# First chunk of an attention and MLP kernel: two loads, masks ahead of the transposes, copies by tile, a third PSUM pair, and unread matmuls in every early gap

## The chip, the cores and the metric

The kernel runs on one core of a Trainium2 chip. Its engines are TensorE (PE, with its weight loads shown apart as PEld), VectorE (DVE), ScalarE (ACT), GpSimd (POOL) and SyncE (SP), and 16 DMA engines move data between HBM and the core's SBUF. Matmuls write to PSUM, which has eight banks of 512 fp32 columns by 128 partitions. The metric is the device time of one execution in microseconds, compared by the median of several runs.

## The reference

Four sequences (B = 4) of 768 positions with 8 heads of 64 go through attention with a window of 128 and 4 sink positions, and then through an MLP over rows of 512:

```python
scores = scale * np.matmul(q, k.transpose(0, 1, 3, 2))
keep = is_sink | in_window                 # first 4 positions, or 0 <= rel < 128
scores = np.where(keep, scores, -1000000000.0)
a = softmax(scores); attn = np.matmul(a, v)
x = attn as [B, S, 512]
xn = (x - mean) / sqrt(var + 1e-6) * g_ln
out = x + np.maximum(xn @ w_ch1, 0.0) @ w_ch2     # w_ch1 512x2048, w_ch2 2048x512
```

Inputs and output are fp32; inside, nearly everything is bf16 with fp32 accumulation.

## The kernel before, in words

**Tiles and chunks.** A tile is 128 query positions of one sequence, a chunk is two tiles (256 positions); there are 12 chunks, three to a sequence. A tile attends to its own 128 keys, to the 128 before them, and, from the third tile on, to the 4 sinks apart. A chunk goes through these stages: loads of k, q and v (POOL issues them, with a cast to bf16), transposes of k and q so that head channels lie on partitions (`kq`), scores, `exp` on ACT, a mask, value matmuls, normalisation and the LayerNorm statistics on DVE, the transpose of the centred rows (`xc` to `xnt`), and two MLP matmuls with a ReLU between them. The MLP weights (`w1`, `w2`, four blocks each) are loaded once, behind the loads of the first chunks.

**The start.** The first four chunks are transposed by PE (`by_dma=4`), later ones by the DMA. For those, `n4` holds k on 64 partitions and q on the other 64, and `tr` (L588 to L593) transposes four heads at a time into one PSUM bank (`pt`, ring `one`), which `evict` (L557) copies to `kq` in one operation of 1024 columns, on ACT or DVE. Chunk 0's loads are cut in half by heads, so that the four loads are k and q of heads 0 to 3, then of heads 4 to 7. Chunks 0 and 1 go through `attend_tile` (L618) tile by tile; from chunk 2 on, `attend` (L670) takes both tiles at once. For tiles 0 and 1 the mask is added in PSUM ahead of the scores: `mk` (L632) multiplies an identity with `neg`, which holds a large negative number where a position is not to be seen, and the scores accumulate on it. `neg` is made on DVE (L490 to L492) from `upper`, which POOL makes with an `affine_select` (L461) behind the first loads. From tile 2 on, the probabilities are multiplied with a 0/1 mask on DVE (L654). `sk` and `sx` (L657 to L663) are the scores of the sinks and their exp, one of each per tile for tiles 2 and 3.

**PSUM.** Two pairs of banks (`pair`) take scores and value sums, four single banks (`one`) the rest.

**What sets the order.** Every operation is recorded in `Plan` with the engines it may run on, a duration that the author gives it, a priority and its buffers. `Plan.run` (L113) lays all of them out in time by these durations: for each engine it picks, among operations that could start within `WINDOW` of the earliest, the one of lowest priority number. It also chooses ACT or DVE where both are possible, and the buffers from the rings. Each engine's instructions are then written in the order of these planned times, and the engine executes them in that order, waiting on semaphores. So a changed duration, priority or ring moves operations on every engine.

**Unread matmuls.** Ahead of 24 us of planned time, gaps of over 0.6 us in PE's plan are filled with matmuls of `junk` into a bank that is free then, whose result nobody reads (L974 to L996); they are 512 columns wide.

Of the kernel before, what the change touches and what calls it, by code (L numbers as in the profile page):

```python
# [7 lines left out]
FP32 = mybir.dt.float32  # L8
BF16 = mybir.dt.bfloat16
# [55 lines left out]
class Plan:  # L65
# [45 lines left out]
    WINDOW = {"PE": 0.4, "ACT": 0.25, "DVE": 0.25, "POOL": 0.25, "SP": 0.0}  # L111

    def run(self):  # L113
        free = {"PE": 0.9, "ACT": 0.75, "DVE": 0.9, "POOL": 1.05, "SP": 0.75}
# [103 lines left out]
SW_4 = (1.4, 0.7, 0.9)  # L218
SW_H = (0.7, 0.8, 0.9)
# [142 lines left out]
def kernel(  # L362
# [38 lines left out]
    pairs = [psum.tile([128, 2, 512], FP32, name=f"pair{i}") for i in range(2)]  # L401
    ones = [psum.tile([128, 512], FP32, name=f"one{i}") for i in range(4)]
    P.ring("pair", [Slot(pairs[i], f"pair{i}", banks[2 * i:2 * i + 2]) for i in range(2)])
    P.ring("one", [Slot(ones[i], f"one{i}", [banks[4 + i]]) for i in range(4)])
# [89 lines left out]
    constant("masks0", "DVE", 0.9, 6.1, masks0, ["upper"], writes=[Bc["mask0"]], nb=20.0)  # L494
# [49 lines left out]
    roots = {}  # L544
# [17 lines left out]
    def load4(c, nm, hs, prio, dma, writes):  # L562
        b, R = c // RC, c % RC
        p0 = 64 * "kq".index(nm)
        ap = (k if nm == "k" else q)[b, hs, 256 * R:256 * R + 256, :].rearrange("h (p i) d -> p h (i d)", i=4)
        P.op(f"{nm}ld{c}{hs.start}", {"POOL": (0.85, 0.9)}, prio, lambda e: G.dma_start(  # L566
            n4_b[c].t[p0:p0 + 64, hs].rearrange("p h i d -> p h (i d)"), ap), writes=writes + [n4_b[c]], dma=dma)

    def chunk(c):
# [5 lines left out]
        if c < PAR["by_dma"]:  # L575
            halves = [[Buf(f"l{c}{hh}{i}") for i in range(2)] for hh in range(2)]
            if c == 0:
                for hh in range(2):
                    for i in range(2):
                        load4(c, "kq"[i], slice(4 * hh, 4 * hh + 4), -110 + hh + 0.1 * i, SW_H, [halves[hh][i]])  # L580
            else:
                for i in range(2):
                    load4(c, "kq"[i], slice(0, H), (PAR["ld1"] if c == 1 else ld) + 0.01 * i, SW_4, [halves[0][i], halves[1][i]])
            for hh in range(2):
                pt, done = Buf(f"pt{c}{hh}", "one"), Buf(f"T{c}{hh}")
                tile_of[c, hh] = done

                def tr(e, pt=pt, hh=hh):  # L588
                    pb = pt.t.bitcast(BF16).rearrange("p (h k i g) -> p h i k g", h=2, k=2, i=4)
                    for h in range(2):  # L590
                        for i in range(4):
                            for h2 in range(2):
                                nc.tensor.transpose(pb[64 * h2:64 * h2 + 64, h, i], n4_b[c].t[:, 4 * hh + 2 * h + h2, i, :], ident)  # L593
                trs[c, hh] = P.op(f"tr{c}{hh}", pe(0.448 if c else 0.9), d + 0.02 + 0.1 * hh, tr, reads=halves[hh] + [Bc["ident"]],
                                  hold=[n4_b[c], T], writes=[pt], mode="c")
                evict(f"ev{c}{hh}", d + 0.05 + 0.1 * hh, 1024,
                      lambda pt=pt: pt.t.bitcast(BF16).rearrange("p (m i g) -> p m g i", m=4, i=4),
                      lambda hh=hh: T.t[:, 2 * hh:2 * hh + 2].rearrange("p h k (g i) -> p (h k) g i", i=4), [pt], [T, done], fp=True)
        else:
            for x, (nm, src) in enumerate((("k", k), ("q", q))):  # L600
                for i in range(2):
                    nat = Buf(f"{nm}n{c}{i}", "nat")
                    ap = src[b, :, 256 * R + 128 * i:256 * R + 128 * (i + 1), :].rearrange("h p d -> p h d")
                    P.op(f"{nm}ld{c}{i}", {"POOL": (0.87, 0.9)}, ld + 0.01 * i + 0.1 * x,
                         lambda e, nat=nat, ap=ap: G.dma_start(nat.t, ap), writes=[nat], dma=SW, after=behind(c))  # L605
                    P.op(f"tr{nm}{c}{i}", {"SP": (1.2, 1.2)}, d + 0.01 * i, lambda e, nat=nat, i=i, x=x: dma_t(
                        T.t[:, :, x, 128 * i:128 * i + 128], nat.t.rearrange("p h d -> p (h d)")),
                        reads=[nat], writes=[T], dma=HW_X, after=[scores[c - 1]])
        if R == 0:
# [4 lines left out]
                for h2 in range(2)], reads=[T], writes=[kts], after=kts_zero)  # L614
# [3 lines left out]
    def attend_tile(t):  # L618
# [4 lines left out]
        need = [[tile_of[cc, hh] for hh in ((j,) if t else (0, 1)) for cc in {c, (t - 1) // 2 if t else 0}]  # L623
                for j in range(2 if t else 1)]
        ps, pp_s = (Buf(f"ps{t}", "ps"), Buf(f"pss{t}", "one")) if c else (None, None)
        pes = []
        for j in range(2 if t else 1):
            pp, pb = Buf(f"s{t}{j}", "pair"), Buf(f"p{t}{j}", "pe")
# [8 lines left out]
            if t < PAR["pm"]:  # L637
                P.op(f"pm{t}{j}", pe(0.44), d + 0.06 + 0.1 * j, mk, reads=[Bc["neg"], Bc["ident"]], writes=[pp],
                     after=[trs[c, 0], trs[c, 1]])

            def sc(e, pp=pp, j=j):
                for hp in (range(2 * j, 2 * j + 2) if t else range(HP)):
# [6 lines left out]
            P.op(f"sc{t}_{j}", pe(0.25), d + 0.1 + 0.1 * j, sc, reads=need[j], **{"rw" if t < PAR["pm"] else "writes": [pp]},  # L649
                 hold=[kq, kprev, pb], mode="r")  # L650
# [5 lines left out]
        if c:  # L656
            def sk(e):  # L657
                for hp in range(HP):
                    nc.tensor.matmul(pp_s.t[32 * hp:32 * hp + 32, 0:128], lhsT=kts_b[0].t[:, hp, :],
                                     rhs=kq.t[:, hp, 1, own], start=True, stop=True, skip_group_check=True)  # L660
            P.op(f"sk{t}", pe(0.21), d + 0.15, sk, reads=[kq, kts_b[0]], writes=[pp_s], hold=[ps], mode="c")
            P.op(f"sx{t}", {"ACT": act(128)}, d + 0.16, lambda e: nc.scalar.activation(
                ps.t[:, own], pp_s.t[:, 0:128], AF.Exp, scale=scale), reads=[pp_s], writes=[ps])  # L663
# [58 lines left out]
    def value(c, i, pes, ps, d, part, srcs):  # L722
        b, R, t = c // RC, c % RC, 2 * c + i
        po = Buf(f"po{t}", "pair")
# [250 lines left out]
    t = 1.2  # L975
    for o in order:
        if o.eng != "PE":
            continue
        if o.start > 24.0:
            break  # L980
        n = int((o.start - t - 0.45) / (0.43 if t < 8 else 0.25))
        if n > 0 and o.start - t > 0.6:
            free = [(max([e_ for b_, e_ in banks[i].lives if b_ < t], default=0.0), i) for i in range(8)
                    if all(e_ < t or b_ > o.start + 0.3 for b_, e_ in banks[i].lives)]
            if free:
                i = min(free)[1]
                items.append((t + 0.001, -n, pairs[i // 2][:, i % 2, :] if i < 4 else ones[i - 4]))
        t = o.start + o.engs["PE"][0]
    items.sort(key=lambda z: (z[0], z[1]))
    with tc.manual_schedule():  # L990
        for _, s, o in items:
            if s < 0:
                for _ in range(-s):
                    nc.tensor.matmul(o, lhsT=junk[:, 0:128], rhs=junk, start=True, stop=True)
# [43 lines left out]
```

## Time and profile before

| what | value |
|---|---|
| median of three runs | 219.2 us (218.75 to 219.54) |
| the profiled execution | 218.84 us |
| its span, first to last instruction | 217.3 us |
| busy in the span: PE, DVE, ACT, POOL | 205.6, 157.1, 118.6, 84.8 us |
| landings of chunk 0's four loads | 5.26, 6.20, 7.13, 8.54 us |
| landings of chunk 1's k and q | 11.25, 13.00 us |
| landings of w1's four blocks | 16.07, 21.20, 23.74, 26.69 us |
| landings of w2's four blocks | 33.52, 35.74, 38.28, 41.01 us |
| first exp starts, first reciprocal starts | 12.13, 13.83 us |

A landing is the moment when a transfer's semaphore tells that all of its bytes are there; the trace gives it as the time from issue to landing. In a timeline row the columns are start and duration in us, engine, line of the code, operation, tiles written and read, shape, count, and in brackets the engine's idle time ahead of it with what ended it. In a row of busy time by stretch they are the stretch and its length, then for PE, PEld, DVE, ACT and POOL the busy us and the number of instructions, then the granted clock of PE, the busy share of the DMA engines and the GB/s that they moved. A chain row gives start, duration and who held the chain. Line numbers are those of the kernel before.

### The profile page before, as it was taken

The numbers are of one execution on the slowest core, as the hardware profiler recorded it, in microseconds if no ns is written. First come the engines' busy times: TensorE is split into PE (matmuls) and PEld (weight loads), VectorE is DVE, ScalarE is ACT, GpSimd is POOL, SyncE is SP. The second block draws the span as 40 slices with busy tenths as digits, with TensorE's granted clock in tenths as the row PEclk, the third lists the DMA queues.
The fourth block names the chain that finished last, engine by engine and source line by source line (L and its number), as shares of the span: only waits on it lengthen the run. The fifth ranks groups of instructions, "written<-read, shape, count | busy, mean of one in ns | idle before, by whom it ended". The sixth has DMA issues, their size and how long they took to land.

```text
span 217.3 us, 5914 instructions
## 1 busy us (share of the span) xinstructions
PE 205.6 (95%) x2378; PEld 167.8 (77%) x2383; DVE 157.1 (72%) x398; ACT 118.6 (55%) x180; POOL 84.8 (39%) x128
## 2 busy tenths in 40 slices
PE   6689999999999799999999999999999999999990
PEld 1447995684697698898897987987988988988880
DVE  3349953499899688689688697787786786794460
ACT  2379577258599756544565555555456456442600
POOL 7968473477039029039057066066110110110000
PEclk9999999999999999999999999999999999999997
DMA  5999999999949949989989939949943520222003
GB/s 48 143 182 202 201 192 207 187 194 147 203 79 108 174 101 90 135 175 99 158 134 130 170 93 140 216 35 141 165 113 48 148 48 0 100 48 94 7 3 109
DMA packets 98098, 26.97 MB, mean 124 GB/s; under 512 B 86800, under 2 KB 94992, under 8 KB 98064
## 3 DMA queue, kind: packets, MB, share of 16 engines
q0 software_dynamic: 66720, 13.64, 78.7%
q1 hardware_dynamic: 31344, 12.89, 31.3%
q8 instruction: 20, 0.33, 0.6%
q14 instruction: 14, 0.11, 0.2%
HBM read 27.30 MB, written 6.29 MB: 155 GB/s over the span
## 4 chain that ended last, share of the span: by engine, by line
PE 85%; DVE 4%; ACT 4%; DMA 2%; issue 1%; POOL 1%; DVEq 0%; ACTq 0%; POOLq 0%
PE one L806 32%; PE one L886 28%; PE one L837 5%; PE one L799 5%; PE pair L734 4%; PE pair L692 4%; DMA n<-in_q_dram 2%; PE pair L729 2%; ACT pe L651 1%; PE one L593 1%; ACT w L948 1%; DVE st L753 1%; POOL n L566 1%; ACT pe L706 1%; PE pair L634 1%
## 5 line engine op out<-in xcount | busy, mean ns | idle before, releaser
L816 ACT ACTIVATE hq<-one 128x512 bf16<-128x512 f32 x93 | 55.4, 598 | 56.1 <-PE one L806 44.9
L806 PE MATMUL one<-xnt,w 128*128 128x256 bf16 x640 | 74.5, 273 | 0.0
L806 PEld LDWEIGHTS <-w 128*128 128x128 bf16 x640 | 61.4, 98 | 7.1
L706 ACT ACTIVATE pe<-pair 128x1024 bf16<-128x1024 f32 (+1 forms) x40 | 36.4, 958 | 22.2 <-PE pair L692 22.2
L761 POOL TENSOR_SCALAR st<-st 128x1 f32<-128x1 f32 x24 | 6.2, 259 | 89.9 <-DVE rec L747 76.7
L886 PEld LDWEIGHTS <-hs 128*128 128x128 bf16 x320 | 30.0, 98 | 5.6 <-issue 1.3
L886 PE MATMUL one<-n,hs 128*128 128x256 bf16 x240 | 29.6, 273 | 0.0
L710 DVE TENSOR_TENSOR pe<-pe,mask 128x1024 bf16<-128x1024 bf16 (+1 forms) x40 | 24.9, 643 | 5.0 <-ACT pe L706 5.0
L900 DVE TENSOR_TENSOR tm<-one,x 128x256 f32<-128x256 f32 x40 | 16.8, 421 | 12.3 <-PE one L886 12.3
L886 PEld LDWEIGHTS <-hq 128*128 128x128 bf16 x240 | 23.3, 98 | 3.0 <-ACT hq L816 0.3
L553 POOL DMA_DIRECT2D vn<-in_v_dram x24 | 21.4, 906 | 4.5 <-DVE xc L764 1.9
L869 DVE TENSOR_TENSOR hs<-hq 128x512 bf16<-128x512 bf16 x40 | 15.4, 413 | 5.4 <-ACT hq L816 5.4
L886 PE MATMUL one<-w,hq 128*128 128x256 bf16 x160 | 19.3, 273 | 0.0
L907 DVE TENSOR_TENSOR ot<-one,tm 128x256 f32<-128x256 f32 x40 | 16.7, 417 | 1.3 <-PE one L886 1.1
L749 DVE TENSOR_TENSOR x<-pair,rec 128x512 bf16<-128x512 f32 x24 | 16.6, 691 | 0.8
L753 DVE BATCH_NORM_STATS2 st<-x 128x6 f32<-128x512 bf16 x24 | 16.6, 690 | 0.4
L799 PE MATMUL one<-xnt,w 128*128 128x128 bf16 x256 | 15.8, 219 | 0.3 <-ACT pe L651 0.3
L605 POOL DMA_DIRECT2D nat<-in_k_dram x16 | 14.8, 924 | 2.6 <-DMA w<-in_moe_w_ch_dram 2.2
L605 POOL DMA_DIRECT2D nat<-in_q_dram x16 | 14.3, 902 | 3.5 <-DMA w<-in_moe_w_ch_dram 3.5
L762 POOL TENSOR_TENSOR st<-st,mhalf 128x1 f32<-128x1 f32 x24 | 14.7, 613 | 2.0
L799 PEld LDWEIGHTS <-w 128*128 128x128 bf16 x256 | 14.5, 98 | 1.0 <-DVE xnt L783 0.5
L837 PE MATMUL one<-w,hq 128*128 128x512 bf16 x60 | 14.8, 380 | 0.2
(86 smaller groups left out, 231.0 us busy)
## 6 DMA issues: line engine op xcount, KB each, us to landing
out_dram<-ot SPq DMA_DIRECT2D x24, 256.0 KB
w<-in_moe_w_ch_dram POOLq DMA_DIRECT2D x8, 512.0 KB, 14.0
vn<-in_v_dram POOLq DMA_DIRECT2D x24, 128.0 KB, 7.3
nat<-in_k_dram POOLq DMA_DIRECT2D x16, 128.0 KB, 5.5
nat<-in_q_dram POOLq DMA_DIRECT2D x16, 128.0 KB, 6.5
n<-in_k_dram POOLq DMA_DIRECT2D x3, 256.0 KB, 13.8
n<-in_q_dram POOLq DMA_DIRECT2D x3, 256.0 KB, 14.6
kq<-nat SPq DMA_TRANSPOSE x32
```

The lines of the kernel that those rows point to most:

```text
L553: P.op(f"vld{t}", {"POOL": (0.87, 0.9)}, prio, lambda e: G.dma_start(bv.t[:, :, 0:64], v[b, :, 128 * r:128 * (r + 1), :].rearrange("h p d ...
L605: lambda e, nat=nat, ap=ap: G.dma_start(nat.t, ap), writes=[nat], dma=SW, after=behind(c))
L706: P.op(f"ex{c}{hp}", {"ACT": act(2 * n)}, d + 0.1 + 0.05 * j, lambda e, pp=pp, pb=pb: nc.scalar.activation(pb.t[:, :, 0:n], pp.t[:, :, 0:n ...
L710: V.tensor_mul(pb.t[:, :, 0:n], pb.t[:, :, 0:n], mm),
L753: P.op(f"bn{t}", {"DVE": fix(0.60)}, d + 0.12, lambda e: V.bn_stats(st.t[:, 8:14], x.t), reads=[x], writes=[st, mv])
L799: nc.tensor.matmul(ph.t[:, 128 * s:128 * s + 128], lhsT=w1[u // 2][:, j, 128 * s:128 * s + 128], rhs=xnt.t[:, j, 128 * (u % 2):128 * (u % ...
L806: nc.tensor.matmul(ph.t[:, 256 * s:256 * s + 256], lhsT=w1[ht // 4][:, j, 128 * (ht % 4):128 * (ht % 4 + 1)], rhs=xnt.t[:, j, :], start=j ...
L816: nc.scalar.activation(hg.t[:, u % 4, :], ph.t, AF.Relu)
L837: nc.tensor.matmul(pc.t[:, 0:wd], lhsT=(hq[s // 2].t[:, (2 * s + i) % 4, 128 * ii:128 * ii + 128] if by_tile else hq[ht // 8].t[:, ht // 2 ...
L886: nc.tensor.matmul(at(r), lhsT=get(left, g)[:, v, s, :], rhs=rhs, start=first and n == 0, stop=n == 7, skip_group_check=True)
L900: return P.op(f"tm{name}_{c}", {"DVE": dve(256, 1.14)}, pr, lambda e: V.tensor_tensor(tm[name].t, at(r), xs[i].t[:, sl], op=ALU.add), read ...
L907: return P.op(f"o{c}_{half}", {"DVE": dve(256, 1.14)}, pr, lambda e: V.tensor_tensor(ots[i].t[:, sl], at(r), tm[name].t, op=ALU.add), read ...
```

## The change

Chunk 0 gets the same two loads as the other chunks, each of all eight heads. The masks of tiles 0 and 1 no longer wait for the transposes, and a ring `first` of three bank pairs, the third made of two banks that are otherwise single, lets all three mask results stand in PSUM at once. Chunk 0's transposes are copied to `kq` in four operations, by bank and by tile, and tile 0's scores need only tile 0's copies. Tile 1's scores are put behind tile 0's. The sinks' scores and exp of tiles 2 and 3 become one operation each. Gaps in PE's early plan are filled down to 0.11 us, with unread matmuls of 512 and then of 128 columns. Several of the plan's numbers change: PE's `WINDOW`, the time at which POOL is free, the durations of loads and of chunk 0's transposes, the earliest time of `masks0`.

In the order in which the engines will execute, PE has ten unread matmuls, six mask matmuls and four unread ones ahead of chunk 0's transposes. Chunk 0's copies stand as two on ACT and two on DVE, where DVE's wait for those of ACT. Behind tile 3's scores the order on PE becomes: values of tile 2, second w1 group, two more w1 groups, the transpose of tile 2's `xc`, values of tile 3, and then the remaining w1 groups. Behind chunk 2 the order of all engines is the old one but for a few neighbours.

```diff
-    WINDOW = {"PE": 0.4, "ACT": 0.25, "DVE": 0.25, "POOL": 0.25, "SP": 0.0}
+    WINDOW = {"PE": 0.3, "ACT": 0.25, "DVE": 0.25, "POOL": 0.25, "SP": 0.0}
...
-        free = {"PE": 0.9, "ACT": 0.75, "DVE": 0.9, "POOL": 1.05, "SP": 0.75}
+        free = {"PE": 0.9, "ACT": 0.75, "DVE": 0.9, "POOL": 1.5, "SP": 0.75}
...
-SW_4 = (1.4, 0.7, 0.9)
-SW_H = (0.7, 0.8, 0.9)
+SW_4 = (1.4, 0.75, 1.0)
...
-    pairs = [psum.tile([128, 2, 512], FP32, name=f"pair{i}") for i in range(2)]
-    ones = [psum.tile([128, 512], FP32, name=f"one{i}") for i in range(4)]
+    low_b = [psum.tile([128, 2, 512], FP32, name=f"pair{i}") for i in range(3)]
+    pairs = low_b[0:2]
+    ones = [low_b[2][:, 0], low_b[2][:, 1]] + [psum.tile([128, 512], FP32, name=f"one{i}") for i in range(2)]
     P.ring("pair", [Slot(pairs[i], f"pair{i}", banks[2 * i:2 * i + 2]) for i in range(2)])
+    P.ring("first", [Slot(low_b[i], f"pair{i}", banks[2 * i:2 * i + 2], rank=i // 2) for i in range(3)])
...
-    def load4(c, nm, hs, prio, dma, writes):
+    def load4(c, nm, prio, loaded):
...
-            halves = [[Buf(f"l{c}{hh}{i}") for i in range(2)] for hh in range(2)]
-            if c == 0:
-                for hh in range(2):
-                    for i in range(2):
-                        load4(c, "kq"[i], slice(4 * hh, 4 * hh + 4), -110 + hh + 0.1 * i, SW_H, [halves[hh][i]])
...
+            loaded = Buf(f"l{c}")
+            for i in range(2):
+                load4(c, "kq"[i], (-110 if c == 0 else PAR["ld1"] if c == 1 else ld) + 0.01 * i, loaded)
...
-                trs[c, hh] = P.op(f"tr{c}{hh}", pe(0.448 if c else 0.9), d + 0.02 + 0.1 * hh, tr, reads=halves[hh] + [Bc["ident"]],
+                trs[c, hh] = P.op(f"tr{c}{hh}", pe(0.46 if c else 0.55), d + 0.02 + 0.1 * hh, tr, reads=[loaded, Bc["ident"]],
                                   hold=[n4_b[c], T], writes=[pt], mode="c")
-                evict(f"ev{c}{hh}", d + 0.05 + 0.1 * hh, 1024,
-                      lambda pt=pt: pt.t.bitcast(BF16).rearrange("p (m i g) -> p m g i", m=4, i=4),
...
+                for i in range(1 if c else 2):
+                    g, done = slice(0, 64) if c else slice(32 * i, 32 * i + 32), Buf(f"T{c}{hh}{i}")
+                    for t in (2 * c, 2 * c + 1) if c else (i,):
+                        tile_of[t, hh] = done
+                    evict(f"ev{c}{hh}{i}", d + 0.05 + 0.1 * hh + 0.2 * i, 1024 if c else 512,
...
-        need = [[tile_of[cc, hh] for hh in ((j,) if t else (0, 1)) for cc in {c, (t - 1) // 2 if t else 0}]
+        need = [[tile_of[t - o, hh] for hh in ((j,) if t else (0, 1)) for o in range(2 if t else 1)]
...
-            pp, pb = Buf(f"s{t}{j}", "pair"), Buf(f"p{t}{j}", "pe")
+            pp, pb = Buf(f"s{t}{j}", "pair" if c else "first"), Buf(f"p{t}{j}", "pe")
...
-                P.op(f"pm{t}{j}", pe(0.44), d + 0.06 + 0.1 * j, mk, reads=[Bc["neg"], Bc["ident"]], writes=[pp],
-                     after=[trs[c, 0], trs[c, 1]])
+                P.op(f"pm{t}{j}", pe(0.44), d + 0.06 + 0.1 * j, mk, reads=[Bc["neg"], Bc["ident"]], writes=[pp])
...
-        if c:
+        if t == 2:
+            pp_s = Buf(f"pss{c}", "one")
+
             def sk(e):
                 for hp in range(HP):
-                    nc.tensor.matmul(pp_s.t[32 * hp:32 * hp + 32, 0:128], lhsT=kts_b[0].t[:, hp, :],
-                                     rhs=kq.t[:, hp, 1, own], start=True, stop=True, skip_group_check=True)
...
+                    nc.tensor.matmul(pp_s.t[32 * hp:32 * hp + 32, 0:256], lhsT=kts_b[0].t[:, hp, :],
+                                     rhs=kq.t[:, hp, 1, :], start=True, stop=True, skip_group_check=True)
...
-    t = 1.2
+    t, was = 1.3, "n"
...
-        n = int((o.start - t - 0.45) / (0.43 if t < 8 else 0.25))
-        if n > 0 and o.start - t > 0.6:
...
+        left = o.start - t - 0.1 - 0.1 * (was != "n") - 0.1 * (o.mode_in != "n" and was != "n")
...
+        if free and left > 0.11:
+            i, nth = min(free)[1], 0
+            to = low_b[i // 2][:, i % 2, :] if i < 6 else ones[i - 4]
+            for n in (512, 128):
+                us = n / (1.2e3 if t < 5.2 else 2.4e3)
+                while left >= us:
+                    items.append((t + 0.001 * (nth + 1), -n, to))
+                    left, nth = left - us, nth + 1
```

## The prediction

> **What bounds the kernel now.** I read the totals first, then the busy time by stretch, then the chain that ended last in order of time, then the timeline of its first 25 us. From the page:
>
> ```profile
> PE 205.6 (95%) x2378; PEld 167.8 (77%) x2383; DVE 157.1 (72%) x398; ACT 118.6 (55%) x180; POOL 84.8 (39%) x128
> ```
>
> Busy time by stretch (columns: PE, PEld, DVE, ACT, POOL, granted clock, DMA share, GB/s):
>
> ```profile
> 0.00:26.00 26.00, 21.22 (x296) 14.01 (x298) 15.25 (x51) 14.59 (x19) 20.15 (x33) 1.00 1.24 154
> 26.00:50.00 24.00, 23.84 (x353) 18.20 (x354) 14.79 (x32) 13.73 (x21) 14.14 (x20) 1.00 1.71 197
> 50.00:100.00 50.00, 48.59 (x517) 39.09 (x516) 42.13 (x105) 34.23 (x58) 21.26 (x31) 1.00 1.33 127
> 100.00:150.00 50.00, 50.00 (x560) 42.88 (x559) 40.16 (x102) 27.17 (x40) 23.87 (x34) 1.00 1.45 136
> ```
>
> From 26 us on PE hardly idles, so the rest is a fixed amount of PE work. What can be won lies ahead of it, and a start that is X us earlier should end X us earlier, as long as nothing else falls due. The chain in order of time shows what sets that start:
>
> ```profile
> 3.59 4.95 DMA n<-in_q_dram
> 8.67 1.06 PE one L593 x16
> 9.73 1.82 PE pair L634 x4
> 11.55 0.97 PE pair L647 x16
> ```
>
> It is the fourth load's landing (8.54), its transposes, the mask matmuls, the scores. The timeline adds durations, PE first:
>
> ```profile
> 1.75 3.59 PE L994 MATMUL pair<-junk 128*128 128x512 bf16 x8 [1.75 <-DVE vn L471]
> 9.67 1.89 PE L634 MATMUL pair<-neg,ident 128*128 128x512 bf16 x4
> ...
> 9.77 1.01 ACT L559 COPY kq<-one 128x1024 bf16<-128x1024 bf16 x1 [1.32 <-PE one L593]
> ...
> 13.28 0.45 PE L734 MATMUL pair<-vn,pe 128*128 128x65 bf16 x8
> ...
> 13.65 0.64 PE L593 MATMUL one<-ident,n 128*64 128x128 bf16 x16
> ...
> 13.83 0.21 DVE L747 RECIPROCAL rec<-pair 128x8 f32<-128x8 f32 x1 [2.67 <-PE pair L734]
> ...
> 14.22 0.61 PE L634 MATMUL pair<-neg,ident 128*128 128x512 bf16 x2
> ```
>
> Sixteen transposes take 1.06 us until about 13 us and 0.64 after; a mask matmul of 512 columns follows the last by 0.43 us before and 0.22 after. PE works at half rate until then. From the reciprocal at 13.83 DVE is nearly full (1.86, 1.48, 1.90, 1.95 and 1.93 busy in the 2-us stretches from 14 to 24), so I measure the start by that reciprocal, the first step behind tile 0's value matmuls.
>
> **The sum's base.** The profiled execution took 218.84 us: span 217.3 and 1.54 around it. The median of the three runs, 219.2, is 0.36 above.
>
> **Two loads instead of four.** POOL issued them for 0.84 + 0.65 + 0.65 + 0.66 = 2.80 us; a whole-head load takes 0.70 (6.75), so two take 1.54 and all that follows on POOL is 1.26 earlier: both selects, every v, k, q and w1 issue. When does the second land? Not before 7.2: the four moved 524 KB; 68 KB by 4.0 as now, the rest at the 186 GB/s of 10:11, ends at 6.45, and the quickest tail, 0.75, I estimate from the first load (its bytes out at about 4.5 by the half-us rates, landed at 5.26). Not after 8.54, if the ramp stays. I take 7.8, the middle: the issue is 1.2 earlier, but the bytes are the same. Transposes start 0.13 after a landing (8.54 to 8.67): 7.93.
>
> **Masks and unread matmuls.** The selects move from 4.30 to 3.05, so the masks' source, done at 6.05 now, is done at 4.8. PE's new list is 7 unread matmuls of 512 and 3 of 128 columns (1.75 to 5.06 at 0.427 and 0.107 us), 6 masks, then 3 of 512 and 1 of 128: 9.25 units of 512 ahead of the transposes. All six masks thereby leave the path. What it costs depends on when PE speeds up: 3.59 us of unbroken work from 1.75 did not do it, and the stretch from 8.67 did it between 12.85 and 13.28, after at most 4.6. Speed at 5.34 frees PE at 7.2, at 6.35 (1.75 + 4.6) at 7.7, never at 5.06 + 9.25 x 0.427 = 9.0. I take 7.7, by the one stretch that shows it; the load then decides, T0 = 7.95.
>
> **From T0 to the reciprocal.** The first copy starts T0 + 0.68 (13.65 to 14.33) and is half as large: 0.60 by the 128x512 row of L816 on ACT. The second bank's copy on ACT runs T0 + 1.35 to 1.95. The built order makes DVE's copies, 0.61 each (half its 1.22), wait for ACT's of the same bank, so the last ends at T0 + 2.6. Tile 0 needs ACT's two only: scores T0 + 2.05, exp 0.48 later (14.76 to 15.24), 1.0 long, done T0 + 3.5. PE meanwhile does tile 1's scores (to T0 + 3.1) and 3 unread matmuls at 0.22 (to T0 + 3.8): the fill costs some 0.2 here. Value matmuls T0 + 3.85, reciprocal 0.55 later (13.28 to 13.83): T0 + 4.4 = 12.35. **Gain 13.83 - 12.35 = 1.48 us.**
>
> **Does the gain survive to 26 us?** ACT: three exps to T0 + 5.6, two chunk-1 copies to T0 + 7.6, two exps (2.05), the sink exp (0.39 by L714 for one of 256, against 0.28 + 0.31), two exps: 20.1, where it now ends 21.76. Chunk 1's transposes stand behind the value matmuls and 0.54 of fill, done when ACT is free. DVE: three tiles' chains (0.2 + 0.69 + 0.69 + 0.18 + 0.35), two evictions of 0.68, four masks of 0.68 from 12.35: last mask 22.75, then PE runs value 3, w1 groups and chunk 2's transposes to 22.85 + 0.75 + 1.8 + 0.9 + 0.22 + 1.8 + 0.9 + 1.02 = 30.24; today it is there at 30.96 with one w1 group (0.9) less done. Gain 1.6; I keep 1.5. The second copy of chunk 2 goes from DVE (1.22) to ACT (1.01), which was busy 13.73 of 24 there: hidden under the two w1 groups that follow. Tile 0's rstd on POOL now stands ahead of the v4, v5 and w2 issues; these landed 11 to 15 us after issue (w2's first 18.5 to 33.5), so the DMA backlog covers that wait.
>
> **Weights.** Landings run in issue order with little room: w1's last block landed 26.69 and PE used it at 26.98; w2's four landed 33.52, 35.74, 38.28, 41.01 and were used at 34.53, 36.90, 39.53, 41.96. So the gain needs the stream to move as well, or stops at 0.95. The stream's lead has bounds 0 and 1.26 (the issues). These rows speak for most of it: after chunk 0 the engines ran short of requests,
>
> ```profile
> 7.50:8.00 0.50, 0.44 (x1) 0.00 (x0) 0.00 (x0) 0.50 (x1) 0.50 (x1) 1.00 2.07 136
> 8.00:8.50 0.50, 0.00 (x0) 0.00 (x0) 0.00 (x0) 0.45 (x1) 0.50 (x2) 1.00 1.23 82
> 8.50:9.00 0.50, 0.33 (x8) 0.36 (x10) 0.00 (x0) 0.00 (x0) 0.50 (x1) 1.00 0.74 72
> ```
>
> and 110 in the next half, against 186: 147 KB, 0.8 us lost, which earlier issues fill. With 0.8 + 0.95 a gain of 1.5 passes. The w1 block is used one group later in the new order (26.5).
>
> **Everything else.** Order on the engines after chunk 2 is the same but for a few swaps of neighbours and buffer names; 0. Sum: 218.84 - 1.5 = 217.35, or 217.7 against the median.
>
> **Rivals.** A, the above: chance 0.50, its own range 217.0 to 218.4.
>
> B, PE speeds up so late that unread work holds the transposes to 8.8 or 9.0: reciprocal 13.2 to 13.4, gain 0.4 to 0.65, time 218.55 to 218.8. For it: 3.59 us were not enough, and a work stretch twice as long may be counted another way. Chance 0.14. The Trainium skill (TensorE: Matmul & The Clock Gate, The HAM clock gate) says that PE is released after one busy window of about 3.4 us which runs free of the kernel. By that rule the rise falls anywhere from 5.16 to 8.57, PE is free between 7.1 and 8.8, and the gain is 0.65 to 1.5; the trace agrees that 3.59 us may be too short.
>
> C, slower: the fill breaks PE's work at the wrong place (masks late, or the wait for the copies at T0 + 1.4 to 2.05) and PE stays at half rate through the first chunks. Then T0 = 9.0, transposes 1.06 each put ACT's second copy at 11.2 to 11.8, scores 11.9, exp 12.5 to 13.5, scores and three fills at 0.43 put the value matmuls at 14.5 and the reciprocal at 15.1: 1.3 later, 220.1 in the profile, 220.5 by the median. It decides once the reciprocal passes 13.83. Against it: the work runs unbroken from 1.75 to T0, longer than the 4.6 that sufficed. Chance 0.14.
>
> D, the weights do not move (POOL's issues wait, or the bytes): gain 0.95, 218.25. Against it is the trough above. Chance 0.12.
>
> E, the load lands at 7.2 and PE is free as early: T0 = 7.35, gain 2.1, 217.1. Chance 0.10.
>
> **Numbers.** 0.3% is 0.66 us, about what this measurement can tell. Faster: A, E, most of D, a little of B: 0.68. Same: most of B, a part of A's and D's edges: 0.15. Slower: C and mishaps of order: 0.17. Range 216.7 to 219.5: it leaves out C's far end and gains above 2.5.
>
> **What would show it.** Second load landed 7.2 to 8.5; masks between 5 and 7.7 with the rate rising among them; first exp at about 10.5 (12.13 now); reciprocal 12.35; w1's last block landed near 25.8; no new PE idle from 26 to 45. Wrong if transposes of chunk 0 take 1.06 each, if PE waits for w blocks, or if the reciprocal moves and the end does not.

## The result, and the profile after

The changed kernel takes 222.19 us (median of four executions, 221.64 to 222.90), the kernel before 219.37 us beside it (218.75 to 220.05). The ratio is 1.013, 95% interval 1.0087 to 1.0173: the change makes the kernel slower by 2.8 us, where 217.7 us and a gain were predicted. The profiled execution took 222.9 us, 221.1 of them its span. Line numbers are now those of each kernel shown, a few lines off those of the kernel before.

The totals of the page, and its share of the chain that ended last by engine:

```profile
PE 207.8 (94%) x2395; PEld 168.5 (76%) x2395; DVE 159.3 (72%) x400; ACT 116.2 (53%) x179; POOL 84.0 (38%) x126
...
PE 79%; DVE 7%; ACT 5%; DMA 3%; issue 2%; POOL 1%; ACTq 0%; POOLq 0%; DVEq 0%
```

PE's share of the chain was 85% before; DVE's and ACT's were 4% each. The busy time by stretch, in the columns of before:

```profile
0.00:26.00 26.00, 21.73 (x316) 15.03 (x317) 16.92 (x54) 13.71 (x18) 19.19 (x31) 1.00 1.34 156
26.00:50.00 24.00, 23.12 (x346) 17.60 (x343) 13.44 (x29) 13.31 (x19) 13.54 (x18) 1.00 1.79 195
50.00:100.00 50.00, 47.66 (x506) 37.88 (x504) 41.51 (x102) 33.62 (x57) 20.17 (x31) 1.00 1.33 126
100.00:150.00 50.00, 49.88 (x554) 42.24 (x553) 40.17 (x102) 26.21 (x40) 23.26 (x33) 1.00 1.27 129
```

In the first 26 us PE is about as busy as before (21.22). What is new lies behind them: PE is idle 0.72 us more from 26 to 50 (23.84 before), 0.93 more from 50 to 100 (48.59) and 0.12 more from 100 to 150 (50.00), and from 50 us on it issues fewer matmuls in each of these stretches.

The chain in order of time, at the start:

```profile
2.44 6.47 DMA n<-in_q_dram
9.04 0.65 PE one L588 x16
9.72 0.59 ACT kq L560
10.33 0.56 DVE kq L560
...
12.08 0.75 PE one L1000 x3
12.83 0.27 PE pair L737 x8
```

The second load is now the first long link; it lands at 8.91 us, later than the fourth of four did (8.54). The masks have left the chain; three unread matmuls (L1000) now stand in it, ahead of tile 0's value matmuls (L737). The timeline of the same stretch, PE, ACT and DVE:

```profile
5.03 2.47 PE L636 MATMUL pair<-neg,ident 128*128 128x512 bf16 x6
...
7.34 0.87 PE L1000 MATMUL one<-junk 128*128 128x512 bf16 x4
...
9.04 1.08 PE L588 MATMUL one<-ident,n 128*64 128x128 bf16 x32 [0.84 <-DMA n<-in_q_dram]
...
9.72 1.07 ACT L560 COPY kq<-one 128x512 bf16<-128x512 bf16 x2 [7.20 <-PE one L588]
...
11.17 2.86 ACT L652 ACTIVATE pe<-pair 128x1024 bf16<-128x1024 f32 x3 [0.38 <-PE pair L648]
...
13.19 0.21 DVE L750 RECIPROCAL rec<-pair 128x8 f32<-128x8 f32 x1 [0.47 <-ACT pe L652]
```

All 32 transposes take 1.08 us, the time that 16 took before: PE is at full rate, and the trace's clock record (the times at which the granted clock changed) has the rise at 7.06 us (13.31 before). The first exp starts 0.96 us earlier, the reciprocal 0.64 us (13.83 before). The start did get faster. Then PE meets waits that it did not have:

```profile
22.01 1.05 PE L802 MATMUL pair<-xnt,w 128*128 128x128 bf16 x16 [0.47 <-ACT hq L819]
...
48.91 1.02 PE L840 MATMUL pair<-w,hq 128*128 128x512 bf16 x4 [0.66 <-ACT kq L560]
...
59.94 1.03 PE L809 MATMUL pair<-xnt,w 128*128 128x256 bf16 x8 [0.43 <-ACT hq L819]
...
67.96 0.39 PE L889 MATMUL pair<-w,hq 128*128 128x256 bf16 x2 [0.54 <-ACT hq L819]
```

Each is a matmul that writes `pair`, and what ended the wait is an ACT operation that reads another result. Before the change these lines wrote `one`: the first and second MLP products live in the ring of single banks. Two of those banks are now `low_b[2][:, 0]` and `low_b[2][:, 1]`, halves of one tile. ACT at the first of these waits:

```profile
20.37 0.59 ACT L819 ACTIVATE hq<-one 128x512 bf16<-128x512 f32 x1
21.36 0.60 ACT L819 ACTIVATE hq<-pair 128x512 bf16<-128x512 f32 x1 [0.40 <-PE pair L802]
```

The ReLU that starts at 21.36 reads the group that PE wrote at 20.27, from one half of the tile. It ends at 21.96, and at 22.01 PE begins the next group, in the other half. The banks differ; the tile is the same.

How far each matched matmul lies behind its counterpart of the kernel before, by the times of the weight loads in two traces (after minus before, us; the time is that of the kernel before; one execution of each):

| kernel | 46 us | 64 us | 105 us | 132 us | 164 us | 207 us |
|---|---|---|---|---|---|---|
| changed | 0.0 | +1.11 | +2.16 | +2.51 | +2.60 | +3.76 |

The lead of the start, 0.43 us at 25 to 28 us, is used up by 46 us, and the loss goes on growing to the end. That was the theory to test, called V in the expectations: the two halves of one PSUM tile wait for each other, all through the kernel. Its rival O: something else in the change, its new order or the unread matmuls, costs the time.

### The profile page after: what moved, and what is told of

It is laid out like the page before. It is cut to its first block, busy times and chain, and to the rows that moved or that the text cites. A ratio compares the mean times of both kernels' runs of the same rounds, so it can differ in the third digit from the quotient of the medians.

```text
span 221.1 us, 5933 instructions
## 1 busy us (share of the span) xinstructions
PE 207.8 (94%) x2395; PEld 168.5 (76%) x2395; DVE 159.3 (72%) x400; ACT 116.2 (53%) x179; POOL 84.0 (38%) x126
## 4 chain that ended last, share of the span: by engine, by line
PE 79%; DVE 7%; ACT 5%; DMA 3%; issue 2%; POOL 1%; ACTq 0%; POOLq 0%; DVEq 0%
PE pair L809 16%; PE one L889 14%; PE one L809 13%; PE pair L889 10%; PE pair L737 4%; PE pair L802 4%; PE pair L695 4%; PE pair L840 3%; PE one L840 3%; DMA n<-in_q_dram 3%; ACT hq L819 2%; PE one L802 2%; DVE hs L872 2%; ACT kq L560 2%; PE pair L732 2%
## 5 line engine op out<-in xcount | busy, mean ns | idle before, releaser
L819 ACT ACTIVATE hq<-pair 128x512 bf16<-128x512 f32 x48 | 27.4, 596 | 40.0 <-PE pair L809 26.7
L764 POOL TENSOR_SCALAR st<-st 128x1 f32<-128x1 f32 x24 | 6.8, 283 | 96.6 <-DVE rec L750 72.5
L809 PE MATMUL pair<-xnt,w 128*128 128x256 bf16 x336 | 41.7, 272 | 0.5 <-ACT hq L819 0.4
L809 PE MATMUL one<-xnt,w 128*128 128x256 bf16 x304 | 38.3, 273 | 0.0
L819 ACT ACTIVATE hq<-one 128x512 bf16<-128x512 f32 x44 | 26.3, 598 | 22.1 <-PE one L809 20.5
L889 PE MATMUL one<-n,hs 128*128 128x256 bf16 x152 | 19.3, 273 | 0.0
L903 DVE TENSOR_TENSOR tm<-one,x 128x256 f32<-128x256 f32 x25 | 10.5, 420 | 6.3 <-PE one L889 6.2
L737 PE MATMUL pair<-vn,pe 128*128 128x65 bf16 x352 | 14.6, 193 | 0.0
L737 PEld LDWEIGHTS <-pe 128*128 128x128 bf16 x352 | 13.8, 97 | 0.9
## 6 DMA issues: line engine op xcount, KB each, us to landing
w<-in_moe_w_ch_dram POOLq DMA_DIRECT2D x8, 512.0 KB, 13.4
```

Of the source, the lines that this page charges most:

```text
L737: nc.tensor.matmul(po.t[:, h // 4, 65 * (h % 4):65 * (h % 4) + 65], lhsT=part(h, n), rhs=vn_b[tv].t[:, h, :], start=(not R and h % 4 == 0 ...
L809: nc.tensor.matmul(ph.t[:, 256 * s:256 * s + 256], lhsT=w1[ht // 4][:, j, 128 * (ht % 4):128 * (ht % 4 + 1)], rhs=xnt.t[:, j, :], start=j ...
L819: nc.scalar.activation(hg.t[:, u % 4, :], ph.t, AF.Relu)
L889: nc.tensor.matmul(at(r), lhsT=get(left, g)[:, v, s, :], rhs=rhs, start=first and n == 0, stop=n == 7, skip_group_check=True)
```

## The experiments: the shared tile

**The shared tile alone, in the kernel before.** Nothing else is touched, and the order on every engine is that of before.

```diff
-    ones = [psum.tile([128, 512], FP32, name=f"one{i}") for i in range(4)]
+    both = psum.tile([128, 2, 512], FP32, name="pair2")
+    ones = [both[:, 0], both[:, 1]] + [psum.tile([128, 512], FP32, name=f"one{i}") for i in range(2)]
```

> The kernel before with one edit: two of the four single banks are now the two halves of one PSUM tile of two banks. No operation is added or moved; every engine's order is that of before. Theory V (waits are set by tile, so an operation on one half waits for the readers and writers of the other): the later growth of the changed kernel comes back alone, from +1.1 us at 64 us to +3.8 at 207, so 221.5 to 223 us, with new waits of PE on ACT's and DVE's reads of the other half. Rival O (the loss is in the order of the operations and in the first chunks): 219.0 to 219.8, no new waits.

Measured: 230.02 us against 219.08, ratio 1.0498 (1.0469 to 1.0527). V's direction is right, and the size is far above what it expected (221.5 to 223): 10.9 us. What PE waited for in that kernel, us in total, times, longest:

```profile
PE pair L887 <- DVE ot L908: 2.7, 4, 0.9
PE pair L887 <- DVE tm L901: 2.1, 4, 0.5
...
PE pair L838 <- ACT kq L560: 0.9, 1, 0.9
PE pair L838 <- DVE ot L846: 0.8, 1, 0.8
```

None of these is among PE's waits of before. The costliest place, on PE and then on DVE:

```profile
205.13 1.03 PE L887 MATMUL pair<-w2t,hq 128*128 128x256 bf16 x8 [0.52 <-DVE tm L901]
206.68 1.03 PE L887 MATMUL pair<-n,hs 128*128 128x256 bf16 x8 [0.52 <-DVE tm L901]
208.23 1.03 PE L887 MATMUL pair<-w,hs 128*128 128x256 bf16 x8 [0.52 <-DVE ot L908]
...
206.21 0.42 DVE L901 TENSOR_TENSOR tm<-pair,x 128x256 f32<-128x256 f32 x1 [0.79 <-PE pair L887]
```

and the same products in the kernel before:

```profile
195.84 1.04 PE L886 MATMUL one<-w2t,hq 128*128 128x256 bf16 x8
196.71 1.04 PE L886 MATMUL one<-n,hs 128*128 128x256 bf16 x8
197.59 1.04 PE L886 MATMUL one<-w,hs 128*128 128x256 bf16 x8
```

Before, the products start 0.87 us apart while DVE reads the one before. With the shared tile they start 1.55 us apart: product, eviction (DVE reads it out), product, eviction, each waiting for the other. Three such steps cost 3 x 0.68 = 2.0 us here alone.

**Two shared tiles in the kernel before.**

```diff
-    ones = [psum.tile([128, 512], FP32, name=f"one{i}") for i in range(4)]
+    both = [psum.tile([128, 2, 512], FP32, name=f"pair{2 + i}") for i in range(2)]
+    ones = [both[i // 2][:, i % 2] for i in range(4)]
```

> The kernel before with its four single-bank PSUM tiles made the halves of two tiles of two banks, not one pair of them alone; order and everything else unchanged. The one shared tile cost 10.9 us. Theory V (each time one half is written while the other is still read, TensorE waits, at many places through the kernel): two shared tiles cost clearly more than one, 15 to 25 us above the kernel before: 234 to 244 us. Rival (the loss sits in a few places that use just these two banks together): within 3 us of the one shared tile, 229 to 233 us.

Measured: 234.98 us against 218.84, ratio 1.0734 (1.0697 to 1.077), 16.1 us above the kernel before and 5.0 above one shared tile. V again, at the low end of its range. Why one shared tile costs 10.9 us here and less in the changed kernel was not looked into.

**The change with its third pair in two tiles.** The third pair becomes a list of two single tiles; the exp that reads it becomes two of 512 columns.

```diff
-    low_b = [psum.tile([128, 2, 512], FP32, name=f"pair{i}") for i in range(3)]
-    pairs = low_b[0:2]
-    ones = [low_b[2][:, 0], low_b[2][:, 1]] + [psum.tile([128, 512], FP32, name=f"one{i}") for i in range(2)]
+    pairs = [psum.tile([128, 2, 512], FP32, name=f"pair{i}") for i in range(2)]
+    ones = [psum.tile([128, 512], FP32, name=f"one{i}") for i in range(4)]
+    low_b = pairs + [ones[0:2]]
...
```

> The changed kernel with the third pair made of two separate tiles of one bank, so that the one exp that reads it becomes two of 512 columns (0.6 us each in place of 1.03). Theory V: the growth behind 60 us is gone and the start's gain of 0.6 at the first reciprocal, less 0.2 for the split exp, remains: 218.5 to 219.2. Rival O: 221.5 to 222.5.

Measured: 217.71 us against 219.08, ratio 0.9941 (0.9918 to 0.9964). The loss is gone and the rest of the change is a gain; V's direction is right, and the time lies below its range (218.5 to 219.2). Busy time by stretch:

```profile
26.00:50.00 24.00, 23.84 (x341) 17.60 (x341) 13.76 (x32) 14.27 (x22) 14.47 (x19) 1.00 1.72 197
50.00:100.00 50.00, 48.34 (x521) 38.97 (x520) 42.56 (x105) 33.55 (x55) 21.82 (x33) 1.00 1.36 127
100.00:150.00 50.00, 50.00 (x562) 42.94 (x560) 40.17 (x101) 27.15 (x40) 23.60 (x33) 1.00 1.35 136
```

From 26 to 50 and from 100 to 150 us PE is as busy as before to the hundredth. Over the whole span PE's busy time falls from 207.8 to 205.1 us, so the waits of the shared tile show only in part as idle time. The table again, with the kernels of this section:

| kernel | 64 us | 105 us | 132 us | 164 us | 207 us |
|---|---|---|---|---|---|
| changed | +1.11 | +2.16 | +2.51 | +2.60 | +3.76 |
| third pair in two tiles | -0.57 | -0.56 | -0.56 | -0.56 | -0.56 |
| before, one shared tile | +3.09 | +3.73 | +5.72 | +6.56 | +10.91 |
| before, two shared tiles | +3.92 | +6.08 | +8.88 | +10.25 | +14.82 |

With the third pair in two tiles the lead stays constant to 0.01 us for 140 us.

**The change without a third pair.** The rings `pair` and `one` are those of before; all else of the change stays.

```diff
...
-    P.ring("first", [Slot(low_b[i], f"pair{i}", banks[2 * i:2 * i + 2], rank=i // 2) for i in range(3)])
...
-            pp, pb = Buf(f"s{t}{j}", "pair" if c else "first"), Buf(f"p{t}{j}", "pe")
+            pp, pb = Buf(f"s{t}{j}", "pair"), Buf(f"p{t}{j}", "pe")
...
```

> The changed kernel with its third pair dropped: two pairs and four tiles of one bank again, so no tile spans two of the four single banks; everything else of the change stays. Theory V (the two halves of one tile wait for each other, all through the kernel): the loss is gone; without a third pair chunk 0's third set of masks has to wait until the exponential has read the first, some 0.4 to 1.0 us on the first chunk, so 217.7 to 218.8 us. Theory O (the rest of the change, its orders and its unread matmuls, costs the time): 221.5 to 222.5 us as the changed kernel.

Measured: 218.10 us against 219.24, ratio 0.9943 (0.9921 to 0.9965). V, within its range; O falls. The third pair, which brought the whole loss, is worth nothing that these runs can tell.

## The experiments: where the gain is

Each of these changes one part of the kernel with the third pair in two tiles (0.9941).

**The old unread matmuls** (the block of before: gaps over 0.6 us, 512 columns; 7 ahead of chunk 1's transposes, where the new rule puts 20).

```diff
...
-        left = o.start - t - 0.1 - 0.1 * (was != "n") - 0.1 * (o.mode_in != "n" and was != "n")
...
+        n = int((o.start - t - 0.45) / (0.43 if t < 8 else 0.25))
+        if n > 0 and o.start - t > 0.6:
...
```

> As split_third, but with the old rule for unread matmuls (gaps over 0.6 us, 512 columns wide). If the dense fill is what brings PE to full rate early, transposes and scores of chunk 0 run at half rate and the first reciprocal comes 0.5 to 1.5 us later than in split_third: 219.2 to 220.2. If the fill only costs time, 218.3 to 218.8.

**No unread matmuls at all.**

```diff
-        if free and left > 0.11:
+        if False and free and left > 0.11:
```

> The kernel with the third pair in two tiles, without any unread matmul; the rest of the order is the same. Theory F (unread matmuls bring the clock up before the first transposes): the rate rises only some time after the transposes have begun, so that 32 transposes take about 2.1 us for 1.08, the scores and the values of tile 0 about twice their time, and the gain of the first chunk is lost by 0.8 to 1.8 us: 218.5 to 219.5 us. Rival (the first chunk goes by its copies and exponentials, on other engines, and the weights' loads hide the rest): 217.3 to 218.1 us.

**Four half loads for chunk 0 again.**

```diff
...
-            for i in range(2):
-                load4(c, "kq"[i], (-110 if c == 0 else PAR["ld1"] if c == 1 else ld) + 0.01 * i, loaded)
+            for hh in range(2 if c == 0 else 1):
+                for i in range(2):
+                    load4(c, "kq"[i], (-110 if c == 0 else PAR["ld1"] if c == 1 else ld) + 0.1 * hh + 0.01 * i, loaded[hh],
+                          slice(0, 8) if c else slice(4 * hh, 4 * hh + 4))
...
```

> As split_third, but chunk 0 is loaded in four half loads as before. If two loads land earlier than four, the second group of transposes starts later than in split_third and the time is 0.3 to 1.0 longer. If one load of twice the size lands no earlier (8.91 in the changed kernel against 8.54 before), the reciprocal is 0.3 to 0.6 earlier: 218.2 to 218.8.

**Masks behind the transposes again.**

```diff
-                P.op(f"pm{t}{j}", pe(0.44), d + 0.06 + 0.1 * j, mk, reads=[Bc["neg"], Bc["ident"]], writes=[pp])
+                P.op(f"pm{t}{j}", pe(0.44), d + 0.06 + 0.1 * j, mk, reads=[Bc["neg"], Bc["ident"]], writes=[pp],
+                     after=[trs[c, 0], trs[c, 1]])
```

> The kernel with the third pair in two tiles, but the masks by matmul wait for the transposes again, as before the change. Theory H (they then lie beside the copies, which take 1.07 us on ScalarE and 1.29 us on VectorE): nothing, 217.4 to 218.1 us. Rival P (at full rate 6 of them take 1.3 us, of which only 4 fit between the transposes and the first scores, and the unread matmuls that are planned in their old place do not replace them): 0.4 to 1.0 us longer, 218.2 to 218.8 us.

**Two whole copies of chunk 0.**

```diff
-                for i in range(1 if c else 2):
-                    g, done = slice(0, 64) if c else slice(32 * i, 32 * i + 32), Buf(f"T{c}{hh}{i}")
+                for i in range(1):
+                    g, done = slice(0, 64), Buf(f"T{c}{hh}{i}")
...
```

> The kernel with the third pair in two tiles, but chunk 0 is copied out of PSUM in two copies of 1024, as before the change, and not in four of 512. Theory C (the scores of tile 0 wait for the copies, and half as much is to be copied for them by tile): first exponential 0.4 to 0.6 us later, and the end by 0.2 to 0.5 us: 217.9 to 218.3 us. Rival N (what comes late is the load, and the second tile's scores or the weights take up the difference): 217.4 to 217.9 us.

| undone, with the third pair in two tiles | median us | ratio to before |
|---|---|---|
| nothing | 217.71 | 0.9941 (0.9918 to 0.9964) |
| old unread matmuls | 217.83 | 0.9969 (0.9936 to 1.0001) |
| no unread matmuls | 217.91 | 0.9944 (0.9919 to 0.9970) |
| four half loads | 218.19 | 0.9968 (0.9948 to 0.9988) |
| masks behind the transposes | 217.46 | 0.9925 (0.9899 to 0.9951) |
| two whole copies | 218.02 | 0.9946 (0.9923 to 0.9969) |

No part, undone alone, changes the time by more than the intervals allow: all overlap that of the first row. With the old unread matmuls the time came out below what either theory expected (218.3 or more), and F, on none at all, fell (217.91 against 218.5 or more); its rival's range holds. P on the masks fell and H holds: behind the transposes they cost nothing that these runs can tell. The four half loads, 0.48 us above the first row, lie within the first expectation (0.3 to 1.0 longer) and at the edge of the second; in the traces the last of the four lands at 8.66 us, the second of two at 8.69, and the reciprocal comes at 12.12 against 12.98. On the copies 218.02 lies in C's range and just above N's, but the intervals do not part them. What C says of the start is in the traces: with two copies the first exp starts 2.73 us behind the first transpose (11.08 - 8.35), with four 2.13 (10.96 - 8.83). The fastest median is that with late masks, 217.46; it beats both kernels of this case, but not demonstrably the other rows.

The no-fill kernel shows why F could be right on its mechanism and wrong on its price. In its profiled execution the clock rose only at 16.89 us:

```profile
8.62 1.92 PE L589 MATMUL one<-ident,n 128*64 128x128 bf16 x32 [0.91 <-DMA n<-in_q_dram]
10.47 0.39 PE L649 MATMUL pair<-kq 64*128 64x128 bf16 x4
11.22 0.82 PE L649 MATMUL pair<-kq 64*128 64x128 bf16 x12 [0.35 <-ACT kq L561]
```

The transposes take 1.92 us instead of 1.08. That execution, 218.89 us, was the slowest of the ten; the fastest, 217.34, is no slower than the fastest of the four with unread matmuls, 217.50.

Then three parts alone, in the kernel before.

**The new unread matmuls alone** (the new block, with the old pairs and single tiles).

```diff
...
+        if free and left > 0.11:
+            i, nth = min(free)[1], 0
+            to = pairs[i // 2][:, i % 2, :] if i < 4 else ones[i - 4]
...
```

> The kernel before with the new rule for unread matmuls alone (all early gaps; 512 and 128 columns). Theory K (the clock is what the first chunk lacks: it rose at 13.31 us in the profile of before, and at 4.5 to 7.4 us wherever the new rule stood in a profile so far): chunk 0's second transposes, masks and scores run at full rate, which takes 1.0 to 1.5 us out of PE's path before the first exponential, and the end comes 0.3 to 0.9 us earlier, 218.2 to 218.8 us. Rival N (each cause alone is hidden by another: the loads, the copies): 218.9 to 219.4 us.

**The masks alone.**

```diff
-                P.op(f"pm{t}{j}", pe(0.44), d + 0.06 + 0.1 * j, mk, reads=[Bc["neg"], Bc["ident"]], writes=[pp],
-                     after=[trs[c, 0], trs[c, 1]])
+                P.op(f"pm{t}{j}", pe(0.44), d + 0.06 + 0.1 * j, mk, reads=[Bc["neg"], Bc["ident"]], writes=[pp])
```

> The kernel before with the masks by matmul no longer held behind the transposes, and nothing else; the planner then puts the 4 masks of the first tile between the transposes of the two load halves. Theory M (4 masks of 1.89 us at half rate leave the path from the second landing to the first scores, of which some 0.8 us stood behind the copies): 0.4 to 1.0 us earlier, 218.1 to 218.7 us. Rival N (copies and weights' loads hide it, as undoing it in the kernel with two tiles cost nothing): 218.8 to 219.4 us.

**The two loads alone.**

```diff
-            if c == 0:
-                for hh in range(2):
-                    for i in range(2):
-                        load4(c, "kq"[i], slice(4 * hh, 4 * hh + 4), -110 + hh + 0.1 * i, SW_H, [halves[hh][i]])
-            else:
-                for i in range(2):
-                    load4(c, "kq"[i], slice(0, H), (PAR["ld1"] if c == 1 else ld) + 0.01 * i, SW_4, [halves[0][i], halves[1][i]])
+            for i in range(2):
+                load4(c, "kq"[i], slice(0, H), (-110 if c == 0 else PAR["ld1"] if c == 1 else ld) + 0.01 * i, SW_4, [halves[0][i], halves[1][i]])
```

> The kernel before with chunk 0's four loads made two, and nothing else. Theory W (two issues fewer on POOL's queue put everything behind them ahead by 0.7 to 1.1 us, the weights' blocks too, and the rest of the early part follows the weights): 0.4 to 1.0 us earlier, 218.1 to 218.7 us. Rival L (the second load lands at 7.7 to 8.9 us in the profiles with two loads, against 8.54 us with four, and now all 32 transposes wait for it at half rate, where 16 were done at 7.3 us): later by 0.3 to 1.0 us, 219.4 to 220.1 us.

| alone, in the kernel before | median us (before 219.02) | ratio to before |
|---|---|---|
| new unread matmuls | 219.58 | 1.0025 (1.0009 to 1.0042) |
| masks ahead | 219.65 | 1.0019 (0.9993 to 1.0044) |
| two loads | 218.48 | 0.9970 (0.9953 to 0.9986) |

Only the two loads gain by themselves. W's range holds and L fell; in the profiled execution, the fastest of its twelve, the matmuls run 0.99 to 1.00 us ahead from 64 to 207 us. K and M fell, and both medians lie above their rivals' ranges too: the new unread matmuls alone make the kernel a little slower (the interval lies above 1), the masks ahead alone cannot be told from nothing. With four half loads the unread matmuls fill a gap, then PE stands still until the second pair lands:

```profile
5.71 0.64 PE L593 MATMUL one<-ident,n 128*64 128x128 bf16 x16
6.28 0.77 PE L997 MATMUL pair<-junk 128*128 128x512 bf16 x5
9.68 1.06 PE L593 MATMUL one<-ident,n 128*64 128x128 bf16 x16 [2.63 <-DMA n<-in_q_dram]
10.68 1.89 PE L634 MATMUL pair<-neg,ident 128*128 128x512 bf16 x4
```

The clock had risen at 5.71 us (16 transposes in 0.64 us) and fell back at 9.12, so that the work behind the late load ran at half rate. This execution, 221.74 us, was the slowest of its thirteen, with a late load (9.55); it shows how the clock can be lost, not what it costs in the median.

What part of the 0.6% of the kernel with separate tiles comes from the two loads (0.3% alone) and what from the rest is not settled: the intervals touch, and undoing the loads alone leaves a gain of 0.3% as well. The merged scores of the sinks and the plan's numbers were not tried alone.

## Why the prediction was wrong, step by step

**The step that failed** is the term "Everything else", put at nothing: "Order on the engines after chunk 2 is the same but for a few swaps of neighbours and buffer names; 0." The order did stay; what changed is which operations may overlap. A line of the diff that makes two single banks views of one tile was read as a name and is worth 4.2 us in this kernel: 1.013 - 0.9941 = 0.019 of 219 us, with the same order on PE, POOL and SyncE and one exp of ACT in two parts. In the kernel before it is worth 10.9 us.

**The base** ("a start that is X us earlier should end X us earlier, as long as nothing else falls due") holds from 64 us on, where the leads are flat in every kernel with separate tiles. It does not hold from the reciprocal, by which the forecast measured the start. In single executions, against the kernel before: with the third pair in two tiles the reciprocal came 0.85 us earlier (12.98) and the matmuls at 207 us 0.56 earlier; without a third pair 2.22 (11.61) and 1.48; with four half loads 1.71 (12.12) and 0.66; with the masks alone in the kernel before 0.52 earlier (13.31), and the matmuls 0.89 later. So what happens between the reciprocal and 64 us is a term of its own. The forecast worked out a gain of 1.6 us at the end of chunk 2's transposes. At their start it was 0.2 in the changed kernel (30.62 us against 29.94, with one w1 group of 0.89 us more done) and 0.9 with the third pair in two tiles (29.91, with that group too).

The forecast named as a sign of its failure "if the reciprocal moves and the end does not", and as a sign of being right "no new PE idle from 26 to 45". The reciprocal moved 0.64 us ahead and the end 2.8 back, and PE was idle 0.72 us more from 26 to 50.

**Two loads: 7.8 us.** Mis-sized for this execution: 8.91, beyond the bound of 8.54. But the landing scatters. In eight profiles of kernels with two loads it was 7.70, 7.79, 8.05, 8.21, 8.31, 8.49, 8.69 and 8.91 (mean 8.27); in six with four it was 7.97 to 9.55 (mean 8.53). The ramp, assumed to stay, does not: GB/s in 0.3-us slices from 0 to 12 us, after and then before,

```profile
GB/s 0 0 0 0 0 0 0 0 3 4 24 43 32 49 127 172 172 178 186 201 191 198 180 163 158 171 180 179 187 124 99 137 142 189 195 182 174 167 154 129
```

```profile
GB/s 0 0 0 0 0 0 0 2 4 1 34 39 99 152 133 135 119 137 167 181 176 172 166 122 137 155 102 79 73 74 90 137 181 190 183 178 192 175 180 166
```

Before, 99 and 152 are reached from 3.6 to 4.2 us, where after has 32 and 49. The trough of before from 7.8 us on (102, 79, 73) is filled (180, 179, 187), as the forecast said. Why the ramp is slower with two loads was not tested.

**Masks and unread matmuls: PE free at 7.7, the load decides.** The load decided. PE's clock rose at 7.06 instead of 6.35, and PE was free at 8.21 (7.34 + 0.87) instead of 7.7, still ahead of the load. A fixed 4.6 us of work is not what raises it: in the seven profiles with the new unread matmuls, all of which start PE at 1.75 us, the rise comes anywhere from 4.46 to 7.35. Rival B's number for the reciprocal nearly came (13.19 against its 13.2 to 13.4), but by the load and not by the clock.

**From T0 to the reciprocal: 4.4 us.** Measured 4.15 (13.19 - 9.04), and 4.15 with separate tiles (12.98 - 8.83). The near hit hides two errors. The first exp started at T0 + 2.13 (11.17) and not 2.53, since the copies and scores took less than was worked out. And the three unread matmuls behind tile 1's scores cost about 0.4 us and not the 0.2 allowed for them: they stand in the chain for 0.75 us (12.08), and with the old unread matmuls in the kernel with the third pair in two tiles, where the first exp starts as far behind T0 (10.58 - 8.45), the reciprocal comes at T0 + 3.75 (12.20). The gain of 1.48 shrank to 0.64 because T0 was 9.04 and not 7.95.

**Weights.** The last block of w1 was forecast at about 25.8: 26.02 after, and a mean of 25.73 in the eight profiles with two loads (26.61 with four, 26.69 before). Right, and the two loads alone bring it (25.56). The last block of w2 came at 40.75 after, and at 40.40 in the mean against 41.35 with four loads (41.01 before).

**The rivals.** C named the direction, slower, but put it on the clock and on a reciprocal past 13.83; the end came later with the reciprocal at 13.19 and the clock up at 7.06. The weights moved, so D did not come, and the load landed after 7.2, so E did not. No rival named the tile.

That the kernel with the third pair in two tiles took 217.71 us where 217.7 was forecast for the change is partly luck. In its one trace (218.23 us, the slowest of its four executions) the load landed at 8.69 and not 7.8, the reciprocal came at 12.98 and not 12.35, and 0.56 of the forecast 1.5 us reached the end. What the faster executions had in its place was not traced.

## What to carry to other kernels

Where a change turns separate PSUM buffers into views of one tile, list every later user of each half, not only the stage for which it was done: the cost falls where one half is written while the other is read. If two banks are wanted as one only for a while, a list of two tiles and one more instruction (here an exp in two of 512 columns) keeps them apart. And a saved issue in a loaded queue has to be counted for everything that stands behind it: here the gain of two loads instead of four showed less in their own landing (0.26 us earlier in the mean) than in the last weight block's (0.88).

## What the runs showed that was not expected

**Two banks in one tile are serialised as one.** One shared tile costs 10.9 us, two 16.1. The waits are the program's: the trace puts them down to the semaphore of the reader of the other half. The Trainium skill (PSUM — Partial Sum Buffer, PSUM bank collisions raise a hardware error) says that engines must be kept apart by bank and quadrant, and that accesses to different banks run clean; here the two halves are different banks, and the kernel with separate tiles runs the same work without these waits. So the waits are more than that rule asks for. Whether a finer way to tell the halves apart within one tile exists was not tried.

**The clock goes by windows, and is lost as it is won.** In the kernel before with its masks ahead, the clock records are: full rate from 4.77 us for 3.413 us, half, full from 11.59 for 6.827, half from 18.42 for 3.413, full from 21.83 for 194.56, half to the end. The granted clock of four stretches shows it (the third column from the right):

```profile
4.00:8.00 4.00, 2.30 (x22) 0.79 (x20) 1.73 (x7) 1.01 (x1) 3.95 (x7) 1.00 1.42 147
8.00:12.00 4.00, 3.14 (x35) 1.95 (x36) 1.40 (x3) 2.23 (x3) 4.00 (x6) 0.57 1.41 152
12.00:16.00 4.00, 3.18 (x72) 2.25 (x72) 2.51 (x7) 3.14 (x4) 2.48 (x4) 1.00 1.59 181
16.00:20.00 4.00, 2.75 (x46) 1.69 (x45) 3.82 (x8) 3.71 (x6) 3.08 (x5) 0.80 1.49 198
```

(The page has 1.00 ahead of the first record, though matmuls then run at half rate.) All of these closed lengths are multiples of 3.413 us (194.56 is 57 of them). The Trainium skill (TensorE: Matmul & The Clock Gate, The HAM clock gate) says that the clock follows the activity in a free-running window of 3413 ns; this trace agrees (3.413, 6.827 = 2 x 3.413). No long pause is needed to lose the rate: between the rise at 11.59 and the fall at 18.42 PE never stood still for longer than in this row, whose pause had only begun:

```profile
18.68 0.61 PE L771 MATMUL one<-ident,xc 128*128 128x128 bf16 x4 [0.80 <-DVE xc L763]
```

So a kernel whose early PE work has holes can meet another rate in another execution: the mean granted clock of the twelve executions of this one lies between 0.971 and 1.0. And unread matmuls that stop ahead of a late load do not hold the rate, as the fall at 9.12 us under a hole of 2.63 us shows (the new unread matmuls alone, above).
